# Two small guards of an attention and gated-MLP kernel change engines: GpSimd to VectorE

## The chip, the cores and the metric

The kernel runs on one core of a Trainium2 chip. The metric is device time in microseconds (us) of one execution. The engines of a core run beside each other, each through its own queue in order: TensorE (matrix products), VectorE, ScalarE, GpSimd, and SyncE, which issues the DMA transfers.

## The reference

Attention over 8 batches of 8 heads, 576 positions and 64 channels, where each position sees itself and the 63 before it; then a gated two-layer network whose gate is a 3-tap convolution along the sequence.

```python
scores = scale * np.matmul(q, k.transpose(0, 1, 3, 2))
mask = (rel >= 0) & (rel < 64)
scores = np.where(mask, scores, -1000000000.0)
attn = np.exp(scores - np.max(scores, axis=-1, keepdims=True))
attn = attn / (np.sum(attn, axis=-1, keepdims=True) + 1e-09)
x = np.matmul(attn, v)          # heads put side by side: (8, 576, 512)
h = np.maximum(x @ w_in, 0.0)   # (8, 576, 1024)
conv_out = conv_w[0] * h[s-1] + conv_w[1] * h[s] + conv_w[2] * h[s+1]
out = (h * sigmoid(conv_out)) @ w_out
```

The weights arrive as 64-bit floats and are turned into 32-bit ones on the chip.

## The kernel before

The 4608 positions are worked in 12 units of 384. A unit has three blocks of scores (`softmax(u, b, ...)`): TensorE makes the scores (`qk`, L350), VectorE masks them and takes the row maxima (`row_max`, L357), ScalarE the exponentials with their sums (`exps`, L367), then the sums get 1e-9 added (`guard`, L370), VectorE takes reciprocals (L373) and the scores are normalised (L378). In units 0 and 1 TensorE transposes the result (`transpose_pe`, L384) and ScalarE copies it out (`untile`, L389). `attend` multiplies with v (L481) and splits the result into two parts of reduced float (`xh`, `xl`, L485 and L488); `moe` does the two layers with three products each (L501, L564).

The weights come in chunks: w_in in pieces 0 and 1 of 128x512 alone, then pairs (2, 3), (4, 5), (6, 7) of 128x1024, and w_out in pairs. Each chunk runs through `weights` and `to_f32`: a load (L264), the absolute value on ScalarE (L248), a lower bound TINY so that the exponent has a floor (L249), a shift on VectorE (L250), the sign (L252), the low word on ScalarE (L255), its addition (L256), a rounded copy on GpSimd (L269), and the remainder on VectorE (L270). A buffer half is loaded again when L256 of its former chunk is done. `weights_conv` puts the small convolution weights through the same steps.

The order on every engine is written by a planner, `queued`, when the program is built. Each piece of work has a due time, a cost in us, and the data that it reads and writes. The planner goes through time and gives each engine, of the works that are ready, the one with the lowest due time:

```python
start = max(free[e], min(x.ready for x in ws))
...
x = min((x for x in waiting[e] if x.ready <= start),
        key=lambda x: x.t - (0.5 if x.kind and x.kind == state[e] else 0.0))
...
y.ready = max(y.ready, end + (0.0 if e == "PE" else 0.06) if y.eng == e else end + 0.2)
```

`at` puts down a work, `two` one that takes the port which VectorE and GpSimd have in common for its whole cost in the plan. The due times stand in a table, START: for unit 0 the exponentials of blocks 0, 1, 2 at -42.377, -37.771 and -19.993 (guard and reciprocal 0.45 later, transposes 0.85 later), the first two w_in pieces at -39.031 and -37.38, the pair (2, 3) at -33.878, and unit 1's first scores at -20.012. Where the plan leaves TensorE idle before 110 us, matrix products on a spare tile (L212) are put in.

Of the kernel before, what the change touches and what calls it, by code (L numbers as in the profile page):

```python
# [8 lines left out]
F32 = mybir.dt.float32  # L9
# [3 lines left out]
ALU = mybir.AluOpType  # L13
# [20 lines left out]
TINY = 2.0 ** -15  # L34
# [127 lines left out]
PORT_CL = 0.5  # L162
# [5 lines left out]
def attention_moe(ctx: ExitStack, tc: tile.TileContext, q, k, v, w_in, conv_w, w_out, out):  # L168
    nc = tc.nc
# [48 lines left out]
    def at(t, eng, cost, do, r=(), w=(), kind=None, mb=0, port=0.0):  # L218

        plan.append(Work(t, eng, cost, do, list(r), list(w), kind, mb, port))  # L220

    def two(t, eng, cost, do, **kw):
        at(t, eng, cost, do, port=cost, **kw)
# [17 lines left out]

    def to_f32(t, n, st, x, kb, kt):

        lw, hw, xu = st[..., 0], st[..., 1], x.bitcast(U32)

        at(t, "ACT", 0.0009 * n + 0.2, lambda: nc.scalar.activation(x, hw.bitcast(F32), AF.Abs), r=kb, w=kt)  # L248
        at(t, "POOL", 0.0027 * n + 0.02, lambda: nc.gpsimd.tensor_scalar(x, x, TINY, None, op0=ALU.max), w=kt, port=PORT_CL)  # L249
        two(t, "DVE", 0.00052 * n + 0.06, lambda: nc.vector.tensor_scalar(  # L250
            xu, xu, 3, 0x3FFFFFF8, op0=ALU.logical_shift_left, op1=ALU.bitwise_and), w=kt)
        two(t, "DVE", 0.00104 * n + 0.07, lambda: nc.vector.scalar_tensor_tensor(  # L252
            xu, hw, 0xC0000000, xu, op0=ALU.bitwise_and, op1=ALU.bitwise_or), r=kb, w=kt)

        at(t, "ACT", 0.0009 * n + 0.2, lambda: nc.scalar.activation(lw, lw, AF.Copy, scale=2.0 ** -29), w=kb)  # L255
        two(t, "DVE", 0.00104 * n + 0.07, lambda: nc.vector.tensor_tensor(xu, xu, lw, ALU.add), r=kb, w=kt)  # L256

    def weights(t, src, fs, hi, lo, key, buf, halves):

        e = slice(halves[0] * DM, (halves[-1] + 1) * DM)  # L260
        st, x = bits[buf][:, e], w24[buf][:, e]
        kb, kt = [("bits", buf, a) for a in halves], [("w24", buf, a) for a in halves]
        for f, a, tl in zip(fs, halves, load_at(buf, halves, t)):
            at(tl, "SP", 0.7, lambda f=f, a=a: nc.sync.dma_start(  # L264
                bits[buf][:, a * DM:(a + 1) * DM], src[f].bitcast(U32).rearrange("p (e two) -> p e two", two=2)),
               w=[("bits", buf, a)], mb=0.52)
        n = len(fs) * DM
        to_f32(t, n, st, x, kb, kt)
        two(t, "POOL", 0.00127 * n, lambda: nc.gpsimd.tensor_copy(hi, x), r=kt, w=[f"{key}{f}h" for f in fs])  # L269
        two(t, "DVE", 0.00104 * n + 0.07, lambda: nc.vector.tensor_tensor(lo, x, hi.bitcast(F32), ALU.subtract),  # L270
           r=kt + [f"{key}{f}h" for f in fs], w=[f"{key}{f}l" for f in fs])

    freed = {}

    def load_at(buf, halves, t):

        ts = [freed.get((buf, a), START["bits"][buf][a]) for a in halves]
        for a in halves:
            freed[(buf, a)] = t + 0.01
        return ts  # L280
# [20 lines left out]
    def wide(u):  # L301
        return u < BY_PE

    def place_of(b, i):

        return divmod(NB * b + i, NT)

    def block(u, b, i):

        first = (u * NT + place_of(b, i)[1]) % SB == 0  # L310
        return (P, W if first else 0, 0) if wide(u) else (KW, 0, 2 if first else 1)
# [25 lines left out]
    def bank_keys(u, b):  # L337
        return {1: [("po", 2), ("po", 3)], 2: [("po", 0), ("po", 1)]}.get(b, [("sc", 0)]) if u == 0 else [("sc", 0)]

    def qk(u, b):  # L340
        rows = W if wide(u) else HW
        for i in range(NB):
            g, t0 = place_of(b, i)
            n, o, _ = block(u, b, i)
            for p in range(2):
                for s in range(0, W, rows):
                    r, t = p * W + s, t0 * W + s
                    for h in range(2):
                        hs = slice(h * D, (h + 1) * D)
                        nc.tensor.matmul(banks_of(u, b)[h][r:r + rows, i * P + o:i * P + n], qs[hs, 2 * g + p, t:t + rows],  # L350
                                         ks[hs, 2 * g + p, t + o:t + n], start=True, stop=True)

    def row_max(u, b):
        for i in range(NB):
            n, o, m = block(u, b, i)
            for h in range(2):
                nc.vector.tensor_tensor_reduce(  # L357
                    out=ss[b][:, i, h, o:n], in0=banks_of(u, b)[h][:, i * P + o:i * P + n], in1=mask[m][:, o:n],
                    scale=-0.125, scalar=3.0e38, op0=ALU.add, op1=ALU.min,
                    accum_out=nms[b][:, 2 * i + h:2 * i + h + 1])  # L360

    def exps(u, b, i):
        n, o, _ = block(u, b, i)
        for h in range(2):
            e = slice(2 * i + h, 2 * i + h + 1)
            x = ss[b][:, i, h, o:n]
            nc.scalar.activation(x, x, AF.Exp, bias=nms[b][:, e], scale=-1.0, accum_out=sms[b][:, e])  # L367

    def guard(b, on):
        on.tensor_scalar_add(sms[b], sms[b], 1e-9)  # L370

    def reciprocal(b):
        nc.vector.reciprocal(rs[b], sms[b])  # L373

    def normalise(u, b, on):
        n = P if wide(u) else KW
        sv = ss[b].rearrange("p t h k -> p (t h) k")[:, :, :n]
        on.tensor_tensor(sv, sv, rs[b].unsqueeze(2).broadcast_to([P, 2 * NB, n]), ALU.mult)  # L378
# [40 lines left out]
    def needed(b):  # L419

        keys = []
        for i in range(NB):
            g, t = place_of(b, i)
            n = int(t >= (4, 2)[g])
            keys += [("q", g, n)] + [("k", g, j) for j in range(n + 1)]
        return list(dict.fromkeys(keys))

    def softmax(u, b, t, ex_at):
        at(t, "PE", 0.90 if wide(u) else 0.82, lambda b=b: qk(u, b), r=needed(b), w=bank_keys(u, b),
           kind="tiled" if wide(u) else "eight")  # L430
        for i in range(NB):
            if block(u, b, i)[1]:
                at(t + 0.1, "POOL", 0.2, lambda b=b, i=i: nc.gpsimd.memset(ss[b][:, i, :, :W], 0.0), w=[("s", b, i)])
        at(t + 0.002, "DVE", 1.69 if wide(u) else 1.45, lambda b=b: row_max(u, b),
           r=bank_keys(u, b) + (["mask0"] if wide(u) else ["mask1", "mask2"]), w=[("s", b, i) for i in range(NB)] + [("nm", b)])
        t = ex_at
        for i in range(NB):
            at(t, "ACT", 0.78 if wide(u) else 0.74, lambda b=b, i=i: exps(u, b, i), r=[("nm", b)],
               w=[("s", b, i), ("sm", b, i)], kind="exp")
        t += 0.45  # L440
        sw = [("sm", b, i) for i in range(NB)]
        if u < 3:
            at(t, "POOL", 0.6, lambda b=b: guard(b, nc.gpsimd), w=sw)
        else:
            at(t, "DVE", 0.15, lambda b=b: guard(b, nc.vector), w=sw)
        at(t, "DVE", 0.15, lambda b=b: reciprocal(b), r=sw, w=[("r", b)])
        sr = [("s", b, i) for i in range(NB)]
        if u < 3:
            two(t, "DVE", 1.15 if wide(u) else 0.88, lambda b=b: normalise(u, b, nc.vector), r=[("r", b)], w=sr)
        else:  # L450
            two(t, "POOL", 1.5, lambda b=b: normalise(u, b, nc.gpsimd), r=[("r", b)], w=sr)
        t += 0.4
        if u < BY_PE:
            for j in range(2):
                m, g = ("po", (2 * b + j) % NC), place_of(b, NB // 2 * j)[0]
                at(t, "PE", 0.66, lambda b=b, j=j: transpose_pe(b, j), r=sr + ["mask0"], w=[m])
                at(t + 0.1, "ACT", 0.55, lambda b=b, j=j: untile(b, j), r=[m], w=[("u", g, i) for i in range(4)])
            return
        t = max(t, when[-1][2] + 0.1)
        for g, t0, rows in parts(b):  # L460
            at(t, "DVE", 0.12 * 2 * len(rows), lambda b=b, g=g, t0=t0, rows=rows: transpose(b, g, t0, rows), r=sr,
               w=[("T", g)] + [("bits", i, a) for i in T_BITS[g] for a in range(2)])
            if t0 + len(rows) == NT:
                if u == BY_PE:
                    at(t + 0.01, "POOL", 1.0, lambda g=g: zero_blocks(g), w=[("u", g, i) for i in range(4)])
                for i in range(4):
                    at(t + 0.05, "SP", 2.1, lambda g=g, i=i: place(g, i), r=[("T", g)], w=[("u", g, i)], mb=0.15)
# [263 lines left out]
```

## Time and profile before

| what | us |
|---|---|
| median of 3 runs | 532.17 (531.51 to 532.33) |
| the profiled execution | 531.34 |
| its span, first to last instruction | 529.6 |
| TensorE matmul busy | 518.5 |
| VectorE busy | 380.3 |
| ScalarE busy | 379.7 |
| GpSimd busy | 112.6 |

Busy time is a sum over the whole span, so it says little about one stretch: TensorE's includes the products on the spare tile. In the rows below, times are us from the span's start unless marked ns; PE is TensorE, PEld its weight loads, DVE is VectorE, ACT ScalarE, POOL GpSimd, SP SyncE; L249 is line 249 of the kernel.

### The profile page before, as it was taken

The numbers are of one execution on the slowest core, as the hardware profiler recorded it, in microseconds if no ns is written. First come the engines' busy times: TensorE is split into PE (matmuls) and PEld (weight loads), VectorE is DVE, ScalarE is ACT, GpSimd is POOL, SyncE is SP. The second block draws the span as 40 slices with busy tenths as digits, with TensorE's granted clock in tenths as the row PEclk, the third lists the DMA queues.
The fourth block names the chain that finished last, engine by engine and source line by source line (L and its number), as shares of the span: only waits on it lengthen the run. The fifth ranks groups of instructions, "written<-read, shape, count | busy, mean of one in ns | idle before, by whom it ended". The sixth has DMA issues, their size and how long they took to land.

```text
span 529.6 us, 14836 instructions
## 1 busy us (share of the span) xinstructions
PE 518.5 (98%) x5826; PEld 499.8 (94%) x5826; DVE 380.3 (72%) x1084; ACT 379.7 (72%) x1011; POOL 112.6 (21%) x196
## 2 busy tenths in 40 slices
PE   9998999999999999999999999999999999999996
PEld 8887889999999999999999999999999999999996
DVE  3899999985858667767767767767767667655552
ACT  2997897579896696696697687687687687544542
POOL 6664467113131011021021021021021021000000
PEclk9999999999999999999999999999999999999999
DMA  8984660237292173183083074073073053010011
GB/s 284 365 296 136 208 231 1 60 109 248 76 325 72 58 256 83 42 291 77 21 297 77 16 253 122 21 285 105 13 264 120 17 152 104 16 61 0 2 60 62
DMA packets 29463, 69.98 MB, mean 132 GB/s; under 512 B 5713, under 2 KB 17617, under 8 KB 29393
## 3 DMA queue, kind: packets, MB, share of 16 engines
q1 hardware_dynamic: 29392, 69.03, 39.7%
q8 instruction: 46, 0.75, 0.6%
q14 instruction: 25, 0.20, 0.1%
HBM read 47.73 MB, written 9.47 MB: 108 GB/s over the span
## 4 chain that ended last, share of the span: by engine, by line
PE 85%; DVE 9%; DMA 1%; ACT 1%; issue 1%; SPq 1%; POOL 0%; DVEq 0%
PE po L564 39%; PE acc L501 36%; PE acc L481 6%; PE sc L350 5%; DVE c L535 1%; DVE w L252 1%; DMA T<-in_w_in_dram 1%; DVE s L357 1%; DVE w L256 1%; DVE wil L270 1%; ACT s L367 1%; SPq L234 1%; DVE xl L488 1%; DVE s L378 1%; DVE w L250 1%
## 5 line engine op out<-in xcount | busy, mean ns | idle before, releaser
L501 PE MATMUL acc<-xh,wih 128*128 128x384 f32 x384 | 131.5, 342 | 0.8 <-DVE xl L488 0.8
L564 PE MATMUL po<-gh,woh 128*128 128x386 f32 (+1 forms) x384 | 132.1, 344 | 0.0
L535 DVE SCALAR_TENSOR_TENSOR c<-hbuf,cw,c 128x386 f32<-128x386 f32 (+1 forms) x192 | 109.6, 623 | 30.7 <-ACT c L528 30.7
L564 PE MATMUL po<-gh,wol 128*128 128x386 f32 (+1 forms) x384 | 129.9, 338 | 0.0
L564 PE MATMUL po<-gl,woh 128*128 128x386 f32 (+1 forms) x384 | 129.7, 338 | 0.0
L501 PE MATMUL acc<-xh,wil 128*128 128x384 f32 x384 | 129.7, 338 | 0.0
L501 PE MATMUL acc<-xl,wih 128*128 128x384 f32 x384 | 129.7, 338 | 0.0
L367 ACT ACTIVATE s<-s,nm 128x96 f32<-128x96 f32 (+2 forms) x288 | 105.1, 367 | 5.2 <-DVE nm L357 4.9
L555 DVE TENSOR_TENSOR gl<-c,gh 128x772 fp32r<-128x772 f32 (+1 forms) x48 | 55.8, 1162 | 28.2 <-ACT gh L551 28.1
L501 PEld LDWEIGHTS acc<-xh,wih 128*128 128x128 f32 x384 | 72.1, 188 | 2.9 <-POOL sm L370 0.7
L564 PEld LDWEIGHTS po<-gh,woh 128*128 128x128 f32 x384 | 72.2, 188 | 2.6
L378 POOL TENSOR_TENSOR s<-s,r 128x768 f32<-128x768 f32 x27 | 39.7, 1472 | 163.5 <-DVE r L373 150.7
L547 DVE TENSOR_TENSOR c<-c,hbuf 128x772 f32<-128x772 f32 (+1 forms) x48 | 47.4, 987 | 36.9 <-ACT c L542 36.7
L564 PEld LDWEIGHTS po<-gl,woh 128*128 128x128 f32 x384 | 72.3, 188 | 0.0
L564 PEld LDWEIGHTS po<-gh,wol 128*128 128x128 f32 x384 | 72.3, 188 | 0.0
L501 PEld LDWEIGHTS acc<-xh,wil 128*128 128x128 f32 x384 | 72.2, 188 | 0.0
L501 PEld LDWEIGHTS acc<-xl,wih 128*128 128x128 f32 x384 | 72.1, 188 | 0.0
L522 ACT ACTIVATE hbuf<-acc 128x384 f32<-128x384 f32 x64 | 30.9, 486 | 45.8 <-PE acc L501 45.4
L542 ACT ACTIVATE c<-c 128x772 f32<-128x772 f32 (+1 forms) x48 | 40.7, 848 | 30.2 <-DVE c L535 29.9
L357 DVE CUSTOM_DVE_ANT_0 s<-sc,mask 128x96 f32<-128x96 f32 (+2 forms) x272 | 51.5, 254 | 9.7 <-POOL mask L321 5.7
L367 ACT ACTIVATION_READ_ACCUMULATOR s<-s,nm 128x1 f32 x288 | 54.3, 189 | 0.0
L511 POOL COPY hbuf<-hbuf 128x4 f32<-128x4 f32 x44 | 16.7, 379 | 176.3 <-DVE c L547 176.2
(64 smaller groups left out, 644.5 us busy)
## 6 DMA issues: line engine op xcount, KB each, us to landing
v<-in_v_dram SPq DMA_DIRECT2D x24, 768.0 KB, 7.2
ub<-T SPq DMA_DIRECT2D x240, 48.0 KB, 1.9
k<-in_k_dram SPq DMA_DIRECT2D x22, 448.0 KB, 4.9
q<-in_q_dram SPq DMA_DIRECT2D x22, 384.0 KB, 6.9
out_dram<-T SPq DMA_DIRECT2D x8, 772.0 KB, 4.2
T<-in_w_in_dram SPq DMA_DIRECT2D x8, 512.0 KB, 6.6
T<-in_w_out_dram SPq DMA_DIRECT2D x8, 512.0 KB, 4.2
out_dram<-T SPq DMA_DIRECT2D x3, 768.0 KB, 6.4
```

Of the source, the lines that this page charges most:

```text
L350: nc.tensor.matmul(banks_of(u, b)[h][r:r + rows, i * P + o:i * P + n], qs[hs, 2 * g + p, t:t + rows], ks[hs, 2 * g + p, t + o:t + n], star ...
L357: nc.vector.tensor_tensor_reduce(out=ss[b][:, i, h, o:n], in0=banks_of(u, b)[h][:, i * P + o:i * P + n], in1=mask[m][:, o:n], scale=-0.125 ...
L367: nc.scalar.activation(x, x, AF.Exp, bias=nms[b][:, e], scale=-1.0, accum_out=sms[b][:, e])
L378: on.tensor_tensor(sv, sv, rs[b].unsqueeze(2).broadcast_to([P, 2 * NB, n]), ALU.mult)
L481: nc.tensor.matmul(acc[bank(("v", u, c))][h * D:(h + 1) * D, t * W:(t + 1) * W], vs[:, c, t, h], ub[g][:, 2 * p:2 * p + 2, 2 * t + h], sta ...
L501: nc.tensor.matmul(acc[bank(("m", u, f))][:, :NX], w[:, f, c], x[u % 2][:, c], start=(c == 0 and j == 0), stop=(c == NC - 1 and j == 2))
L522: nc.scalar.activation(hbuf[:, f, o:o + NX], ps[:, :NX], AF.Relu)
L535: nc.vector.scalar_tensor_tensor(c, hbuf[:, f, e:e + n], cw[:, e, f:f + 1], c, op0=ALU.mult, op1=ALU.add)
L542: nc.scalar.activation(c, c, AF.Sigmoid)
L547: nc.vector.tensor_tensor(c, c, hbuf[:, 2 * i:2 * i + 2, 1:1 + n], ALU.mult)
L555: nc.vector.tensor_tensor(gls[ring(u, i)][:, :, :n], cs[i % 2][:, :, :n], ghs[ring(u, i)][:, :, :n].bitcast(F32), ALU.subtract)
L564: nc.tensor.matmul(po[o][:, :n], w[:, f, es], x, start=(f == 0 and j == 0), stop=(f == NF - 1 and j == 2))
```

## The change

The 1e-9 of unit 0's three blocks, and the lower bound TINY of the two w_in pieces that are converted alone, are done by VectorE. Units 1 and 2 keep GpSimd for the 1e-9 (the later units had VectorE already), and the other chunks keep GpSimd for TINY. The costs given to the planner go with the engines; all due times stay. Since the order is planned from costs, the order of other works may come out otherwise too.

```diff
-    def to_f32(t, n, st, x, kb, kt):
+    def to_f32(t, n, st, x, kb, kt, early=False):
...
-        at(t, "POOL", 0.0027 * n + 0.02, lambda: nc.gpsimd.tensor_scalar(x, x, TINY, None, op0=ALU.max), w=kt, port=PORT_CL)
+        if early:
+            two(t, "DVE", 0.00052 * n + 0.06, lambda: nc.vector.tensor_scalar(x, x, TINY, None, op0=ALU.max), w=kt)
+        else:
+            at(t, "POOL", 0.0027 * n + 0.02, lambda: nc.gpsimd.tensor_scalar(x, x, TINY, None, op0=ALU.max), w=kt, port=PORT_CL)
...
-        to_f32(t, n, st, x, kb, kt)
+        to_f32(t, n, st, x, kb, kt, len(fs) == 1)
...
-        if u < 3:
+        if 0 < u < 3:
             at(t, "POOL", 0.6, lambda b=b: guard(b, nc.gpsimd), w=sw)
         else:
             at(t, "DVE", 0.15, lambda b=b: guard(b, nc.vector), w=sw)
```

## Rows read from the trace of the kernel before

**Rows 1.** Busy time by stretch: length, each engine's busy time (instructions), clock, DMA.
```profile
12.30:19.25 6.95, 6.23 (x80) 6.01 (x79) 3.89 (x8) 6.95 (x31) 2.98 (x4) 1.00 1.04 410
19.25:38.40 19.15, 18.11 (x320) 16.35 (x317) 18.97 (x68) 18.67 (x66) 13.71 (x13) 1.00 0.86 301
38.40:75.84 37.44, 33.35 (x453) 30.52 (x454) 37.41 (x89) 31.79 (x84) 20.00 (x16) 1.00 0.60 198
```

**Rows 2.** TensorE's waits from 76 us on: total, times, longest.
```profile
PE acc L501 <- DVE xl L488: 0.2, 1, 0.2
```

**Rows 3.** Timeline 12 to 19 us: start, length, engine, line, operation.
```profile
12.29 0.67 ACT L248 ACTIVATE w<-T 128x512 f32<-128x512 f32 x1 [4.56 <-DMA T<-in_w_in_dram]
...
13.05 1.49 POOL L249 TENSOR_SCALAR w<-w 128x512 f32<-128x512 f32 x1 [2.97 <-ACT w L248]
...
14.57 0.43 DVE L250 TENSOR_SCALAR w<-w 128x512 uint32<-128x512 uint32 x1 [2.14 <-POOL w L249]
...
15.03 0.69 DVE L252 SCALAR_TENSOR_TENSOR w<-T,w 128x512 uint32<-128x512 uint32 x1
15.07 0.19 ACT L367 ACTIVATION_READ_ACCUMULATOR s<-s,nm 128x1 f32 x1
...
15.34 0.50 POOL L370 TENSOR_SCALAR sm<-sm 128x8 f32<-128x8 f32 x1 [0.80 <-ACT s L367]
...
15.87 0.20 DVE L373 RECIPROCAL r<-sm 128x8 f32<-128x8 f32 x1
...
16.10 1.22 DVE L378 TENSOR_TENSOR s<-s,r 128x1024 f32<-128x1024 f32 x1
...
17.25 0.68 DVE L256 CUSTOM_DVE_ANT_0 w<-T,w 128x1024 uint16<-128x1024 uint16 x1
...
17.77 1.00 PE L350 MATMUL sc<-k,q 64*64 64x128 f32 x32 [0.72 <-DMA q<-in_q_dram]
...
18.64 0.69 DVE L270 TENSOR_TENSOR wil<-w,wih 128x512 fp32r<-128x512 f32 x1 [0.71 <-POOL wih L269]
...
18.70 1.09 PE L384 MATMUL po<-ident,s 128*128 128x128 f32 x8
```

**Rows 4.** Timeline 18 to 29 us, three engines, by engine.
```profile
18.69 0.68 ACT L248 ACTIVATE w<-T 128x512 f32<-128x512 f32 x1
...
19.88 1.16 ACT L248 ACTIVATE w<-T 128x1024 f32<-128x1024 f32 x1
20.94 0.57 ACT L389 COPY ub<-po 128x512 f32<-128x512 f32 x1
...
21.12 2.96 POOL L249 TENSOR_SCALAR w<-w 128x1024 f32<-128x1024 f32 x1
...
19.25 0.28 DVE L357 CUSTOM_DVE_ANT_0 s<-sc,mask 128x128 f32<-128x128 f32 x1
...
20.80 0.08 DVE L357 DVE_READ_ACCUMULATOR2_ANT nm<- 128x1 f32 x1
21.03 0.43 DVE L250 TENSOR_SCALAR w<-w 128x512 uint32<-128x512 uint32 x1
...
21.49 1.41 DVE L252 SCALAR_TENSOR_TENSOR w<-T,w 128x512 uint32<-128x512 uint32 x1
22.82 1.21 DVE L378 TENSOR_TENSOR s<-s,r 128x1024 f32<-128x1024 f32 x1
...
23.95 0.68 DVE L256 CUSTOM_DVE_ANT_0 w<-T,w 128x1024 uint16<-128x1024 uint16 x1
...
29.06 1.21 DVE L256 CUSTOM_DVE_ANT_0 w<-T,w 128x2048 uint16<-128x2048 uint16 x1
```

**Rows 5.** Timeline at 123 us, VectorE: a later unit's guard and reciprocal.
```profile
123.05 0.16 DVE L370 TENSOR_SCALAR sm<-sm 128x8 f32<-128x8 f32 x1
123.24 0.20 DVE L373 RECIPROCAL r<-sm 128x8 f32<-128x8 f32 x1
```

**Rows 6.** Timeline at 38 us, VectorE: a later normalisation.
```profile
38.20 2.06 DVE L378 TENSOR_TENSOR s<-s,r 128x1024 f32<-128x1024 f32 x1
```

More of the change, by code (lines that the diff above doesn't have):

```diff
@@ L267, in weights @@
         n = len(fs) * DM
-        to_f32(t, n, st, x, kb, kt)
-        two(t, "POOL", 0.00127 * n, lambda: nc.gpsimd.tensor_copy(hi, x), r=kt, w=[f"{key}{f}h" for f in fs])
-        two(t, "DVE", 0.00104 * n + 0.07, lambda: nc.vector.tensor_tensor(lo, x, hi.bitcast(F32), ALU.subtract),
-           r=kt + [f"{key}{f}h" for f in fs], w=[f"{key}{f}l" for f in fs])
+        to_f32(t, n, st, x, kb, kt, len(fs) == 1)
+        his, los = [f"{key}{f}h" for f in fs], [f"{key}{f}l" for f in fs]
+        two(t, "POOL", 0.00127 * n, lambda: nc.gpsimd.tensor_copy(hi, x), r=kt, w=his)
+        two(t, "DVE", 0.00104 * n + 0.07, lambda: nc.vector.tensor_tensor(lo, x, hi.bitcast(F32), ALU.subtract), r=kt + his, w=los)
     freed = {}
```

## The prediction

> **What bounds the kernel now.** I read the busy time by stretch first [rows 1]. From 19.25 us to 38.40 VectorE works 18.97 of 19.15 us, and from 38.40 to 75.84 it works 37.41 of 37.44, so it is full. Before that, from 12.30 to 19.25, it works only 3.89 of 6.95 us. TensorE's granted clock is 1.00 in all three, the upper of its two levels (2.4 GHz), so the clock is no term here. Then I read TensorE's waits behind 76 us: there is one, 0.2 us long, for VectorE [rows 2]. So the start-up is set by VectorE until about 76 us, and then TensorE alone sets the pace. A change that lies before 42 us, as this one does, can only move the moment at which TensorE becomes free of VectorE; microseconds won before it must survive a full VectorE queue.
>
> Third, the order of time around the first weight chunk [rows 3]. ScalarE starts its absolute value at 12.29, GpSimd's guard runs from 13.05 for 1.49 us, and VectorE, which has been idle for 2.14 us, goes on at 14.57. The first score block's sums are complete at 15.07 + 0.19 = 15.26; GpSimd guards them from 15.34 and VectorE's reciprocal starts at 15.87. Fourth, the same around the second chunk [rows 4].
>
> **The first chunk's exponent.** Removed: 1.49 us of GpSimd. Added: a VectorE tensor_scalar over 128x512 with one constant. No row shows it in float; the nearest is the shift at L250, same shape and engine, which lets the next instruction go 0.34 us after it (21.03 to 21.37) [rows 4]. Bounds: 0.34, and 0.69 if it ran as slowly as the two-input L252 [rows 3]; I take 0.34. It starts where GpSimd did (13.05), so the shift goes from 14.57 to 13.39, and L252 ends near 14.4 instead of 15.7. That 1.2 us is worth nothing by itself: what VectorE has to do next is the sums' guard, and ScalarE delivers those at 15.26 as before. The later chain is set by the normalisation.
>
> **The first block's sums.** A guard on VectorE with the reciprocal behind it takes 0.19 us from start to start (123.05 to 123.24) [rows 5]. From the same 15.34: reciprocal at 15.53 instead of 15.87, normalisation at 15.76 instead of 16.10. Gain: 0.34 us, bounded by 0 and the 0.53 that GpSimd's part takes now (15.34 to 15.87). Everything tied to it follows: L256 at 16.91, and with the 1.39 us from L256 to L270 (17.25 to 18.64, GpSimd's cast between them), L270 at 18.30, out of the way 0.61 later at 18.91.
>
> **What that does to the written order.** The planner takes, of the works that are ready, the one with the earliest due time. The transposes of block 0 are due at -41.5, the scores of unit 1's block 0 at -20.0. In the run TensorE took the scores first, at 17.77, when their q had landed, and the transposes at 18.70 [rows 3]. The normalisation now takes 0.15 + 0.15 + 1.15 by its costs instead of 0.6 + 0.15 + 1.15, and one allowance of 0.2 for a hop between engines becomes 0.06: 0.59 sooner by the planner's clock. I worked its rule through by hand: the transposes become ready just ahead of the load (by 0.1 on its clock, which serves here for the order alone). So I expect the transposes first, from about 17.0 to 18.1, and the scores right behind. Then VectorE finds block 1's sums (at 18.87, as now, because ScalarE's exponentials don't move) ready before unit 1's scores, and does guard, reciprocal and normalisation of block 1 ahead of the row maxima; now they stand at 21.37 and 22.82, behind them.
>
> **The second chunk.** On VectorE, by the same row distances: guard 18.91, reciprocal 19.10, normalisation 19.33, out at 20.48 (1.15, as 16.10 to 17.25); row maxima 1.63 (19.25 to 20.88), out at 22.11; exponent guard 22.45; shift 22.79; L252 with 0.62 unhindered, 23.41. At present the same work, the normalisation at 22.82 included, is out at 23.95 [rows 4]. Lead: 0.54 us. GpSimd's wait at 21.03 bought nothing before: VectorE was in the row maxima until 20.88, so its removal is worth 0.15 at most.
>
> **The port.** At 21.12 GpSimd starts its guard of chunks 2 and 3, and L252 at 21.49 takes 1.41 us instead of 0.69 [rows 3, 4]: 0.72 lost. A normalisation that starts just behind such a guard takes 2.06 instead of 1.21 [rows 6, 3]. With both copies of unit 0's block 0 (0.47 each, 20.94 to 21.41 in spacing) now ahead of ScalarE's two absolute values, that guard starts near 21.47. L252 was freed at 21.12 + 1.09; the same would hold VectorE to 22.56, and the new guard at 22.11 could lose 0 to 0.45. No row has a one-input VectorE instruction beginning under a GpSimd instruction, so I keep both and take 0.2 between. What reads against a dearer collision is the normalisation at 22.82: it began inside the 2.96 us of the GpSimd guard (21.12 to 24.08) and took its plain 1.21 [rows 4]. The Trainium skill, "SBUF — State Buffer", section "Who interferes with whom", says that a VectorE instruction in a two-port mode or with two SBUF inputs and a GpSimd instruction exclude each other for the whole of the one that issued first. By it that normalisation would have stood until 24.08; the row disagrees. By the rule the sum below would grow by some 2 us; by the row it does not.
>
> **From 23.41 on.** The same set of work up to the end of unit 1's second row maxima takes 23.95 to 29.06 now, 5.11 us [rows 4]. It gains the third block's guard, 0.19; its GpSimd form lay beside other work, so nothing on VectorE pays for it. The lead is 0.54 - 0.2 - 0.19 = 0.15, between -0.1 (full collision) and 0.35 (none). The third chunk and the rest keep their code. L256 of chunk 1 probably falls behind the second row maxima, so its buffer's reload on SyncE's queue and, one in-order queue on, chunk 4's absolute value come nearly 1 us later. The plan can fill that gap on ScalarE with exponentials. Without that cover the late value would cost VectorE up to the same 1 us.
>
> **Sum.** The profiled execution took 531.34 us (span 529.6 and 1.7 around it), the median of the three runs is 532.17, 0.83 above. 531.34 - 0.15 = 531.2 for the profiled one, 532.17 - 0.15 = 532.0 for the median. About 1.06 us (0.2%) is what a measurement of this kernel can tell from no change.
>
> **The rivals.** *No lead at all*: the transposes stay behind the scores. Then the row maxima still wait for qk, the second chunk's guard falls at 20.9 and L252 meets GpSimd at the same place; 0.19 for the third guard remains: 532.2 to 532.4. For it: the margin of 0.1. Chance 0.10. *Faster*: the shifted queues miss collisions that are there now. Each is worth 0.72 to 0.85 [rows 4, 6]; the full lead of 0.35 with one or two of them is -1.2 to -2.05, 530.1 to 531.0. For it: VectorE is full, so each stall lost there comes through; against it: GpSimd waits for the same VectorE and ScalarE results, so its starts move along. Chance 0.27. *Slower by the order*: the due times belong to the old durations. It is the reload of chunk 1's buffer: if ScalarE's queue has chunk 4's absolute value ahead of unit 1's exponentials, all behind it comes up to 1 us later, and one more collision of 0.85 follows when GpSimd's guard meets a normalisation; +1.5 to +1.9, 533.7 to 534.0. It decides once the delay exceeds the time that VectorE has other ready work. Chance 0.23. *Slower by the port*: the new fast instruction at 22.11 stands until the GpSimd guard that began at 21.47 has ended, 2.96 us on, at 24.43: 2.32 lost, less 0.35 of lead, 534.1. Beside it stands the skill's page named above; the row at 22.82 speaks against it, though it has another shape. Chance 0.08.
>
> **How the numbers follow.** Forecast 0.32 and no lead 0.10 make 0.42 within 0.2%; faster 0.27; slower 0.23 + 0.08 = 0.31. The forecast's own range is 531.3 to 532.9, with the bounds of the lead and one collision either way cut at the threshold. The range takes in both sides: from 530.1, two collisions missed, to 534.0, the reload and one collision; what is beyond it is most of the port case and a third collision.
>
> **What the changed profile would show.** The first shift near 13.4; the first reciprocal near 15.5; L384 ahead of unit 1's first L350 on TensorE; block 1's normalisation before 19.5; a VectorE guard near 22.1 of 0.34 to 0.8 us; the second L256 after L357 of unit 1's second block. VectorE still full from 20 to 76 us, and TensorE's last wait for VectorE near 75.7. I would be wrong if VectorE gets holes behind 24 us, if the new guard lasts above 2 us, if TensorE's order changes between 38 and 76 us so that it waits in other places, or if the transposes stay behind the scores and still something moves.

## The result, and the profile after

The changed kernel took 533.64 us (median of 13 runs) beside 532.17 for the kernel before; the ratio is 1.0032, with a 95% interval from 1.0023 to 1.0042. One of the 13 runs of the kernel before took 1749.32 us and is not in the ratio, which compares the runs that agree. So the change is slower, by 1.5 us by the medians and by some 1.7 by the ratio. The range on record (530.1 to 534.0) holds it; the forecast "within 0.2%" does not.

The profiled execution took 533.82 us. Lines behind the edit have moved by one to four: L250 is the new lower bound on VectorE, L253 the shift (L250 before), L255 the sign (L252), L259 the addition of the low word (L256), L274 the remainder (L270), L353 the scores (L350), L360 the row maxima (L357), L370 the exponentials (L367), L373 the guard (L370), L381 the normalisation (L378), L387 the transposes (L384), L484 the product with v (L481), L491 `xl` (L488), L504 and L567 the two layers (L501, L564), L521 and L525 ScalarE's copies of the first layer's output out of PSUM (L518, L522), L538 the convolution (L535), L558 the low part `gl` that the second layer reads (L555). `nm` are the row maxima, `wil` and `wol` the remainders of w_in and w_out.

First the place of the edit. Timeline of the changed kernel, 13 to 32 us, VectorE: start, length, engine, line, operation.

```profile
13.60 0.43 DVE L250 TENSOR_SCALAR w<-w 128x512 f32<-128x512 f32 x1 [0.48 <-ACT w L248]
14.06 0.43 DVE L253 TENSOR_SCALAR w<-w 128x512 uint32<-128x512 uint32 x1
...
15.90 0.17 DVE L373 TENSOR_SCALAR sm<-sm 128x8 f32<-128x8 f32 x1 [0.69 <-ACT s L370]
16.11 0.20 DVE L376 RECIPROCAL r<-sm 128x8 f32<-128x8 f32 x1
16.42 1.23 DVE L381 TENSOR_TENSOR s<-s,r 128x1024 f32<-128x1024 f32 x1
17.56 0.68 DVE L259 CUSTOM_DVE_ANT_0 w<-T,w 128x1024 uint16<-128x1024 uint16 x1
...
20.00 1.23 DVE L381 TENSOR_TENSOR s<-s,r 128x1024 f32<-128x1024 f32 x1
21.14 0.42 DVE L250 TENSOR_SCALAR w<-w 128x512 f32<-128x512 f32 x1
21.48 0.28 DVE L360 CUSTOM_DVE_ANT_0 s<-sc,mask 128x128 f32<-128x128 f32 x1
...
23.03 0.42 DVE L253 TENSOR_SCALAR w<-w 128x512 uint32<-128x512 uint32 x1
23.49 0.69 DVE L255 SCALAR_TENSOR_TENSOR w<-T,w 128x512 uint32<-128x512 uint32 x1
...
27.21 0.58 DVE L373 TENSOR_SCALAR sm<-sm 128x8 f32<-128x8 f32 x1
27.71 1.21 DVE L255 SCALAR_TENSOR_TENSOR w<-T,w 128x1024 uint32<-128x1024 uint32 x1
...
31.11 1.21 DVE L259 CUSTOM_DVE_ANT_0 w<-T,w 128x2048 uint16<-128x2048 uint16 x1
```

The new bound frees the shift 0.46 us after it starts, not 0.34, and the guard frees the reciprocal after 0.21. (In this execution ScalarE began the first absolute value at 12.90, 0.61 later than in [rows 3]; read distances here, not start times.) Block 1's normalisation stands at 20.00, ahead of the row maxima, and L255 takes 0.69 where it took 1.41 [rows 4]. Up to here it goes much as forecast. TensorE's timeline confirms the other step on which the forecast rested, transposes ahead of scores:

```profile
17.79 1.06 PE L387 MATMUL po<-ident,s 128*128 128x128 f32 x8 [0.29 <-DVE s L381]
18.79 1.00 PE L353 MATMUL sc<-k,q 64*64 64x128 f32 x32
```

Now where the time went. I counted how many weight products of the two layers TensorE had started by a given time (instructions of L504 and L567, of L501 and L564 before; all 2304 are in each trace). Between 90 and 110 us the kernel before starts 114 of them in 20 us, so one is worth 0.175 us. The last column counts the instructions on the spare tile (L212) between 50 and 110 us, which stand where the plan leaves TensorE idle. The five lower rows are experiments, told below.

| kernel | by 50 us | by 66 | by 90 | by 110 | spare products |
|---|---|---|---|---|---|
| before | 33 | 72 | 179 | 293 | 40 |
| after | 48 | 72 | 177 | 286 | 62 |
| e2: order of after, engines of before | 48 | 72 | 178 | 286 | 62 |
| e1: engines of after, order of before | 30 | 72 | 176 | 290 | 40 |
| e5: before, one planned cost changed | 36 | 72 | 166 | 273 | 66 |
| e11: before, other due times | 48 | 89 | 209 | 312 | 28 |
| e12: the same order, engines of after | 37 | 84 | 203 | 310 | 28 |

At 50 us the changed kernel is 15 products ahead (2.6 us); at 66 it is level, at 110 it is 7 behind (1.2 us). So the loss does not come from the edit's own place; it comes behind 50 us. The starts of single products, later (+) or earlier (-) than in the kernel before, show its parts (one execution each, from TensorE's timelines; e7 and e10 are experiments that repair the first part):

| weight product | before, us | after | e2 | e1 | e7 | e10 |
|---|---|---|---|---|---|---|
| 37th | 50.62 | -3.72 | -3.52 | +0.48 | -3.05 | -4.60 |
| 241st | 100.80 | +0.35 | +0.25 | +0.49 | +0.02 | -1.70 |
| 301st | 111.38 | +1.25 | +1.15 | +0.50 | +0.96 | -0.06 |
| 541st | 165.97 | +2.43 | +2.45 | +0.46 | +2.12 | +1.09 |

From the 541st on the changed kernel stays some 2.4 us late, which is the difference of the two spans (532.0 and 529.6). First its lead is used up. Then 0.9 us go before the 301st product, where six spare products stand that the kernel before doesn't have:

```profile
103.25 0.82 PE L212 MATMUL acc<-spare 128*128 128x112 f32 x6
```

The last 1.2 us go between the 301st and the 541st, where TensorE waits in neither kernel: these 240 products take 54.6 us in the kernel before and e1, and 55.7 to 55.9 in the changed kernel, e2 and e7 to e10, which have its order of TensorE there. The same eight sets of products with v and five of scores stand among them in nine groups instead of six. No experiment shows whether changing between these kinds of product costs the whole 1.2 us.

For the first part, the windows of the changed kernel show the stretch from 40 us on (length, busy time of PE, PEld, DVE, ACT, POOL with their instructions, TensorE's clock, DMA share, GB/s):

```profile
40.00:54.00 14.00, 13.15 (x148) 11.63 (x148) 13.97 (x33) 13.72 (x32) 6.61 (x5) 1.00 0.32 98
54.00:58.00 4.00, 2.38 (x89) 1.81 (x83) 4.00 (x21) 1.39 (x4) 2.11 (x1) 0.94 0.48 193
58.00:62.00 4.00, 4.00 (x18) 4.00 (x18) 4.00 (x6) 3.98 (x8) 0.65 (x3) 0.64 0.76 211
62.00:66.00 4.00, 4.00 (x59) 3.72 (x65) 4.00 (x21) 4.00 (x10) 3.23 (x2) 1.00 0.54 215
```

TensorE's own timeline says what happens between 54 and 66 us:

```profile
54.52 0.47 PE L212 MATMUL po<-spare 128*128 128x112 f32 x2
56.62 1.32 PE L353 MATMUL sc<-k,q 64*32 64x96 f32 x64 [1.62 <-DVE nm L360]
57.87 0.69 PE L504 MATMUL acc<-xh,wih 128*128 128x384 f32 x1
58.36 0.52 PE L504 MATMUL acc<-xh,wil 128*128 128x384 f32 x1
58.68 0.52 PE L504 MATMUL acc<-xl,wih 128*128 128x384 f32 x1
...
61.45 1.26 PE L212 MATMUL po<-spare 128*128 128x112 f32 x10
```

It waits 1.62 us for row maxima. Behind the wait, twelve products take 57.87 to 61.45, 0.30 us each instead of 0.175: the granted clock has gone to its lower level (0.64 on average in that window). Then come spare products, because the plan has nothing ready. VectorE's timeline shows what it waits for: four steps of the convolution (51.56, 3.77 us) stand ahead of the row maxima. It also shows two works that have become late: the remainder of the chunk (6, 7), 57.73 now and 51.81 before, and an `xl` of unit 1. Three of the four `xl` were done at 70.1 before and the last came at 75.24; now two are done at 66.5, and the other two come at 74.53.

```profile
51.56 3.77 DVE L538 SCALAR_TENSOR_TENSOR c<-hbuf,cw,c 128x386 f32<-128x386 f32 x4
55.25 0.25 DVE L360 CUSTOM_DVE_ANT_0 s<-sc,mask 128x96 f32<-128x96 f32 x1
...
57.73 1.21 DVE L274 TENSOR_TENSOR wil<-w,wih 128x1024 fp32r<-128x1024 f32 x1
...
71.54 1.23 DVE L259 CUSTOM_DVE_ANT_0 w<-T,w 128x2048 uint16<-128x2048 uint16 x1 [1.31 <-ACT T L258]
72.68 1.93 DVE L538 SCALAR_TENSOR_TENSOR c<-hbuf,cw,c 128x386 f32<-128x386 f32 x2
74.53 1.01 DVE L491 TENSOR_TENSOR xl<-acc,xh 128x384 fp32r<-128x384 f32 x2
```

The same places in the kernel before, VectorE and then TensorE:

```profile
51.81 2.05 DVE L270 TENSOR_TENSOR wil<-w,wih 128x1024 fp32r<-128x1024 f32 x1
53.78 1.14 DVE L535 SCALAR_TENSOR_TENSOR c<-hbuf,cw,c 128x386 f32<-128x386 f32 x2
54.85 0.25 DVE L357 CUSTOM_DVE_ANT_0 s<-sc,mask 128x96 f32<-128x96 f32 x1
...
69.13 1.01 DVE L488 TENSOR_TENSOR xl<-acc,xh 128x384 fp32r<-128x384 f32 x2
...
75.24 0.55 DVE L488 TENSOR_TENSOR xl<-acc,xh 128x384 fp32r<-128x384 f32 x1
...
53.57 0.41 PE L501 MATMUL acc<-xh,wih 128*128 128x384 f32 x1
56.22 1.16 PE L350 MATMUL sc<-k,q 64*32 64x96 f32 x64 [0.31 <-DVE nm L357]
```

The row maxima begin only 0.40 us later than before (55.25 and 54.85). The wait is long because TensorE is early: the twelve products that it had for this time before (from 53.57) are already done. So the lead of 15 products ends here, because VectorE does not bring the row maxima forward. GpSimd has a part in that, by the new order: two of the convolution's steps take 1.10 us at 48.27, the four take 3.77 while GpSimd rounds the chunk (6, 7) and guards the next one (timeline of the changed kernel, GpSimd):

```profile
51.70 1.37 POOL L273 CAST wih<-w 128x1024 fp32r<-128x1024 f32 x1 [6.43 <-DVE w L259]
53.03 3.08 POOL L252 TENSOR_SCALAR w<-w 128x1024 f32<-128x1024 f32 x1
```

The convolution's due times (1.5, 3.5, 5.5) are far later than the chunk's (-12); it stands ahead because the planner takes only works that are ready. The remainder needs GpSimd's rounded copy of its chunk, which ran at 49.77 before and runs at 51.70 now, when VectorE is free and the convolution ready.

### The profile page after: what moved, and what is told of

It is laid out like the page before. It is cut to its first block, busy times and chain, and to the rows that moved or that the text cites. A ratio compares the mean times of both kernels' runs of the same rounds, so it can differ in the third digit from the quotient of the medians.

```text
span 532.0 us, 14850 instructions
## 1 busy us (share of the span) xinstructions
PE 522.6 (98%) x5836; PEld 502.7 (94%) x5836; DVE 380.3 (71%) x1089; ACT 379.7 (71%) x1011; POOL 105.4 (20%) x191
## 4 chain that ended last, share of the span: by engine, by line
PE 89%; DVE 7%; DMA 1%; SPq 1%; ACT 1%; issue 0%; POOL 0%; DVEq 0%
PE po L567 39%; PE acc L504 37%; PE acc L484 6%; PE sc L353 5%; DMA T<-in_w_in_dram 1%; DVE s L381 1%; DVE s L360 1%; PE po L212 1%; DVE c L538 1%; DVE w L259 1%; SPq L234 1%; DVE wil L274 1%; DVE w L255 1%; ACT s L370 0%; DVE xl L491 0%
## 5 line engine op out<-in xcount | busy, mean ns | idle before, releaser
L538 DVE SCALAR_TENSOR_TENSOR c<-hbuf,cw,c 128x386 f32<-128x386 f32 (+1 forms) x192 | 111.5, 633 | 31.0 <-ACT c L531 31.0
L504 PE MATMUL acc<-xh,wih 128*128 128x384 f32 x384 | 132.3, 345 | 1.2 <-ACT hbuf L525 0.6
L567 PE MATMUL po<-gh,woh 128*128 128x386 f32 (+1 forms) x384 | 132.3, 345 | 0.0
L504 PE MATMUL acc<-xh,wil 128*128 128x384 f32 x384 | 130.5, 340 | 0.0
L504 PE MATMUL acc<-xl,wih 128*128 128x384 f32 x384 | 130.2, 339 | 0.0
L567 PE MATMUL po<-gh,wol 128*128 128x386 f32 (+1 forms) x384 | 130.0, 338 | 0.0
L567 PE MATMUL po<-gl,woh 128*128 128x386 f32 (+1 forms) x384 | 129.9, 338 | 0.0
L370 ACT ACTIVATE s<-s,nm 128x96 f32<-128x96 f32 (+2 forms) x288 | 105.1, 367 | 6.0 <-DVE nm L360 5.8
L504 PEld LDWEIGHTS acc<-xh,wih 128*128 128x128 f32 x384 | 72.7, 189 | 3.8 <-issue 1.1
L558 DVE TENSOR_TENSOR gl<-c,gh 128x772 fp32r<-128x772 f32 (+1 forms) x48 | 54.9, 1144 | 28.6 <-ACT gh L554 28.6
L567 PEld LDWEIGHTS po<-gh,woh 128*128 128x128 f32 x384 | 72.3, 188 | 2.6
L381 POOL TENSOR_TENSOR s<-s,r 128x768 f32<-128x768 f32 x27 | 39.7, 1471 | 168.6 <-DVE r L376 168.6
L567 PEld LDWEIGHTS po<-gl,woh 128*128 128x128 f32 x384 | 72.4, 188 | 0.3 <-DVE gl L558 0.3
L504 PEld LDWEIGHTS acc<-xh,wil 128*128 128x128 f32 x384 | 72.6, 189 | 0.0
L504 PEld LDWEIGHTS acc<-xl,wih 128*128 128x128 f32 x384 | 72.6, 189 | 0.0
L567 PEld LDWEIGHTS po<-gh,wol 128*128 128x128 f32 x384 | 72.4, 188 | 0.0
L525 ACT ACTIVATE hbuf<-acc 128x384 f32<-128x384 f32 x64 | 30.9, 483 | 40.5 <-PE acc L504 40.5
L360 DVE CUSTOM_DVE_ANT_0 s<-sc,mask 128x96 f32<-128x96 f32 (+2 forms) x272 | 51.6, 255 | 11.3 <-PE sc L353 11.2
L531 ACT ACTIVATE c<-hbuf,cw 128x386 f32<-128x386 f32 (+1 forms) x96 | 53.6, 608 | 1.2 <-DVE gl L558 1.2
L370 ACT ACTIVATION_READ_ACCUMULATOR s<-s,nm 128x1 f32 x288 | 54.4, 189 | 0.0
```

The costliest lines, as they stand in the source:

```text
L360: nc.vector.tensor_tensor_reduce(out=ss[b][:, i, h, o:n], in0=banks_of(u, b)[h][:, i * P + o:i * P + n], in1=mask[m][:, o:n], scale=-0.125 ...
L504: nc.tensor.matmul(acc[bank(("m", u, f))][:, :NX], w[:, f, c], x[u % 2][:, c], start=(c == 0 and j == 0), stop=(c == NC - 1 and j == 2))
L525: nc.scalar.activation(hbuf[:, f, o:o + NX], ps[:, :NX], AF.Relu)
L531: nc.scalar.activation(cs[i % 2][:, a, :n], hbuf[:, f, 1:1 + n], AF.Copy, scale=cw[:, 1, f:f + 1])
L538: nc.vector.scalar_tensor_tensor(c, hbuf[:, f, e:e + n], cw[:, e, f:f + 1], c, op0=ALU.mult, op1=ALU.add)
L558: nc.vector.tensor_tensor(gls[ring(u, i)][:, :, :n], cs[i % 2][:, :, :n], ghs[ring(u, i)][:, :, :n].bitcast(F32), ALU.subtract)
```

## The experiments

Theory A: the engines are worth nothing that can be told; the loss is the other order that the planner writes from the new costs. Theory B: the work itself on VectorE costs it (a full engine, or the port shared with GpSimd). Each kernel was timed in five rounds beside the kernel before, whose median was 531.28 us in e1 to e4, 531.68 in e5 to e8, 531.82 in e9 to e11 and 531.53 in e12; medians below are therefore compared by their ratios to it.

**e1: the engines without the order.** VectorE does the three kinds of work, but the planner is still given GpSimd's cost and queue, so every other work keeps its place. (e2 is the reverse: the planner is told VectorE, the instruction is issued by GpSimd.)

```diff
         if early:
-            two(t, "DVE", 0.00052 * n + 0.06, lambda: nc.vector.tensor_scalar(...), w=kt)
+            at(t, "POOL", 0.0027 * n + 0.02, lambda: nc.vector.tensor_scalar(...), w=kt, port=PORT_CL)
...
-        if 0 < u < 3:
-            at(t, "POOL", 0.6, lambda b=b: guard(b, nc.gpsimd), w=sw)
+        if u < 3:
+            at(t, "POOL", 0.6, lambda b=b: guard(b, nc.gpsimd if u else nc.vector), w=sw)
```

> VectorE does the five guards, but the planner is still given GpSimd and GpSimd's costs for them, so every queue keeps the order of before. Theory A (the order is what costs): not slower than before, 531.2 to 532.4 in the median, VectorE's remainder of w_in chunk (6, 7) done near 54 us as before, TensorE's clock 1.00 throughout. Theory B (five more instructions on a full VectorE and their meetings with GpSimd at the port cost): 533 to 534, with VectorE falling behind before by about 1 us from 21 us on.

531.74 us, ratio 1.0006 (0.9997 to 1.0016): no difference that can be told. The timeline of e1, VectorE, shows why nothing was won either: the second chunk's shift now meets GpSimd's guard of the chunks (2, 3) (0.92 us instead of 0.43), and L259 starts at 24.14, where it started at 23.95 [rows 4].

```profile
21.44 0.92 DVE L253 TENSOR_SCALAR w<-w 128x512 uint32<-128x512 uint32 x1
22.29 0.19 DVE L376 RECIPROCAL r<-sm 128x8 f32<-128x8 f32 x1
22.40 0.69 DVE L255 SCALAR_TENSOR_TENSOR w<-T,w 128x512 uint32<-128x512 uint32 x1
23.01 1.22 DVE L381 TENSOR_TENSOR s<-s,r 128x1024 f32<-128x1024 f32 x1
24.14 0.68 DVE L259 CUSTOM_DVE_ANT_0 w<-T,w 128x1024 uint16<-128x1024 uint16 x1
```

**e2: the order without the engines.**

> The planner is given the change's engines and costs, so every queue has the order of after, but GpSimd does the five guards as before. Theory A (the order): slower than before by at least what the change costs, 533.6 to 535.5, the more because GpSimd's 1.5 us guards stand in a plan made for 0.3 us. Theory B (VectorE's load): as before, 531.5 to 532.5.

533.53 us, ratio 1.0042 (1.0029 to 1.0055): the whole loss, with all the moved guards on GpSimd. In the two tables above its counts and delays are nearly those of the changed kernel, and the wait for the row maxima is the same (TensorE's waits from 30 to 130 us in e2: total, times, longest):

```profile
PE sc L353 <- DVE nm L360: 1.6, 1, 1.6
```

e1 and e2 together decide for Theory A: the order is enough to make the loss, the engines are not.

**e3 and e4: one half of the change each**, engines and planned costs together: e3 moves the sums' guards alone, e4 the exponents' bounds alone.

```diff
e3:  -        to_f32(t, n, st, x, kb, kt, len(fs) == 1)
e3:  +        to_f32(t, n, st, x, kb, kt)
e4:  -        if 0 < u < 3:
e4:  +        if u < 3:
```

> Only the three sums' guards of unit 0 move to VectorE, in cost and engine. Theory A: this alone brings the transposes of block 0 ahead of unit 1's scores and the normalisation of block 1 ahead of the row maxima, so the w_in chunk (6, 7) is late again and the time is 533 to 535. Theory C (the first chunk's exponent, 1.2 us sooner, is what upsets the order): as before, 531.5 to 532.5.

> Only the lower bounds of w_in chunks 0 and 1 move to VectorE, in cost and engine. Theory A: the first sums still decide when block 0 is normalised, so the first 20 us keep the order of before; 531.7 to 532.7. Theory C: the order breaks here, 533 to 535.

e3: 533.2 us, 1.0031 (1.0021 to 1.0041). One detail of Theory A is not there: the remainder of the chunk (6, 7) came at 50.67, as early as before, so that late piece is not a necessary part of the loss. e4: 534.95 us, 1.0064 (1.005 to 1.0077). Under Theory A I had expected little of it; it is slower than the whole change. The theory was right that the order decides, and I was wrong on which edit disturbs it. Both halves break the order, each in another way, and their losses do not add up to that of the whole.

**e5: no engine moved at all.** The kernel before, with the planner told that unit 0's guard on GpSimd costs 0.5 us instead of 0.6 (it takes 0.50 for the first block [rows 3], and 0.55 and 1.10 for the other two).

```diff
-            at(t, "POOL", 0.6, lambda b=b: guard(b, nc.gpsimd), w=sw)
+            at(t, "POOL", 0.5 if u == 0 else 0.6, lambda b=b: guard(b, nc.gpsimd), w=sw)
```

> The kernel before, every operation on its old engine; only the planner's cost for unit 0's guard on GpSimd is 0.5 instead of 0.6, a tenth of a microsecond in the plan. Theory A (the due times fit one set of costs, and any other order that they give is worse): slower than before by 1.5 to 4 us, with the queues in another order from the first guard on. Theory D (the changed engines' order alone is bad, a nudge of costs is harmless): as before, within 0.6 us.

535.69 us, 1.008 (1.0067 to 1.0093), 4 us slower by 0.1 us in one planned cost. Its spare products rise to 66. The due times fit one set of costs; another set, though truer for the first block, loses microseconds.

**e6: the change with other due times.** A search tries due times in START one after another and keeps those with which the written plan ends sooner.

```diff
-    "sig": ((3.087, 7.079, 8.764, 10.751), ...
-    "in": (-39.031, -37.38, -33.878, -12.682, -12.013),
+    "sig": ((5.041, 7.079, 8.764, 8.969), ...
+    "in": (-39.031, -37.38, -33.878, -14.293, -12.377),
...
```

> The change with other due times, found by a search on the planner's own clock with the change's costs; the operations and the data flow are those of the change. Theory A: the loss is a matter of due times, so it goes away: no slower than before, 528.5 to 531.5, with the w_in chunk (6, 7) back before 55 us. Theory B (the moved instructions cost VectorE time that no order gives back): still 1 us or more above before, 532.3 and up.

529.34 us, 0.996 (0.9946 to 0.9973): faster than both kernels. But the remainder of the chunk (6, 7) still came at 57.22, and TensorE still waited 1.57 us at 56.11; so this order does not repair what I had found late, and the expectation that it would is wrong. The gain comes behind 58 us, where weight products fill what spare products held. Whether the change or the search earns it is the question of e11.

**e7: the hole at 55 us filled**, that is, the 1.62 us in which TensorE waits for the row maxima. Seven spare products (14 instructions in the trace) in place of one where the plan is at 55.3.

```diff
-            n = int((start - t) * FILL)
+            n = 7 if 55.2 < t < 55.4 else int((start - t) * FILL)
```

> The change, with seven spare products instead of one where TensorE stands 1.6 us before unit 2's third scores, so that it stays busy there. If the lowered clock behind that hole (the granted clock was 0.64 in 58 to 62 us) is a part of the loss, it stays at 1.00 and the time falls by 0.4 to 1.3 us against the change: 532.0 to 533.0. If the clock is no part, the time stays or grows by up to 0.3 us, and a low clock shows elsewhere or none did cost.

532.56 us, 1.0017 (1.0008 to 1.0026). TensorE's wait for `nm` shrinks from 1.62 to 0.26 us, the clock is 1.00 in all windows from 54 to 80 us, and about half of the loss is gone, though the spare products do no work. So part of it was the low clock behind the wait, as far as the intervals tell, which just overlap with those of the changed kernel. In its profiled execution the 241st product is level with the kernel before; the two later parts of the loss are there as in the changed kernel (0.94 and 1.16 us).

**e8 and e9: the stretch behind 66 us.** e8 puts no spare products behind 66 us of the plan; e9 adds one edit, the two `xl` of unit 1 moved ahead of the convolution's works due 5.5 in VectorE's queue.

```diff
e8:  -FILL, FILL_FROM, FILL_TO = 4.0, 2.0, 110.0
e8:  +FILL, FILL_FROM, FILL_TO = 4.0, 2.0, 66.0
...
e9:  -        for x in queued(plan, keep_busy):
e9:  +        order = queued(plan, keep_busy)
e9:  +        los = [x for x in order if x.w in ([("xl", 1, 0)], [("xl", 1, 3)])][:2]
e9:  +        for x in los:
e9:  +            order.remove(x)
e9:  +        i = next(i for i, x in enumerate(order) if x.eng == "DVE" and x.t == 5.5)
e9:  +        order[i:i] = los
e9:  +        for x in order:
```

> The change without the spare products that the planner puts in behind 66 us of its clock: 18 rows near 69 us and 6 near 103 us. If these products hold up work that is ready (the remainder of w_out's first chunk is done at 69.2 us and its first product starts at 71.2), the time falls by 0.6 (those near 103 alone) to 2.5 us against the change. If they only fill waits, it stays, and an idle TensorE may lower the clock and cost 1 us more.

> The kernel of e8_no_late_filler with one edit of order more: the two VectorE splits of unit 1's values c0 and c3 (xl, the low parts that the weight products of unit 0's f=6 and f=7 read) stand in VectorE's queue right before the first work of the conv whose due time is 5.5, instead of behind it and behind the second exponents. Theory (TensorE at 70 to 75 us is short of work because these two splits come at 74.5 us while their inputs are ready at 69.8): TensorE's wait of 1.85 us at 75.4 us for xl goes, the granted clock of 74 to 80 us comes back from 0.72 to 1.00, and the time falls by 1.3 to 2.5 us against e8, to 531.0 to 532.2 us. Rival (the late splits only show where TensorE has run dry; something else before 66 us sets it): the wait moves to another tile and the time stays at 533.2 to 533.8 us.

e8: 533.47 us, 1.0037 (1.0024 to 1.005), nothing won. The second layer starts at 69.5 instead of 71.2, but what the spare products had covered comes out as a wait for the late `xl` (TensorE, timeline of e8), and the clock goes to 0.72 in the window 74 to 80:

```profile
75.45 0.44 PE L504 MATMUL acc<-xh,wih 128*128 128x384 f32 x1 [1.85 <-DVE xl L491]
```

e9: 532.4 us, 1.0017 (1.0005 to 1.0029), 1.07 less than e8. The `xl` now stand at 69.92, that wait is gone and the clock of 74 to 80 us is 1.00. So the late `xl` are a second part, again with intervals that just overlap. The gain is a little below the 1.3 to 2.5 expected: in the profile of e9 TensorE waits later instead, 0.98 us at 97.00 for `gl`, and 1.38 at 104.65 for ScalarE's copy out of PSUM, where the changed kernel has its six spare products:

```profile
97.00 0.44 PE L567 MATMUL po<-gl,woh 128*128 128x386 f32 x1 [0.98 <-DVE gl L558]
104.65 0.45 PE L504 MATMUL acc<-xh,wih 128*128 128x384 f32 x1 [1.38 <-ACT hbuf L521]
```

**e10: both repairs**, the filled hole of e7 and the order of e9.

> e9_splits_first with the hole at 55 us filled as in e7_hole_filled (7 spare products in the place of 1). Theory (the hole with its low clock and the late splits are two separate losses that add up): e7 was worth 1.1 us, so e10 comes out about 1.1 us under e9, at 530.0 to 531.2 us, under the kernel before's 531.7. Rival (both are the same microseconds of slack of TensorE, lost once): e10 is within 0.4 us of e9.

532.65 us, 1.0023 (1.0012 to 1.0033): no faster than e9. The expectation that two losses add up is wrong. The hole's wait is down to 0.27 us here, but TensorE waits 1.16 at 68.71 for the remainder of a w_out chunk, 0.45 at 95.10 for `gl`, and 1.39 at 102.75 for ScalarE's copy. What is repaired early is taken back later: the 241st product starts 1.70 us ahead of the kernel before, the 301st level with it (that last wait), the 541st 1.09 us behind (the order of TensorE, as in the changed kernel). So what e9 and e10 leave of the loss lies behind 100 us.

**e11: the control of e6.** The kernel before, guards on GpSimd, with due times from the same search.

```diff
-    "bits": ((-46.561, -47.419), (-44.383, -45.007)),
-    "qk1": -43.011,
+    "bits": ((-46.561, -47.419), (-44.383, -47.12)),
+    "qk1": -44.246,
...
-    "ex0": (-42.377, -37.771, -19.993),
+    "ex0": (-42.377, -34.695, -19.993),
...
```

> The kernel before, guards on GpSimd as they were, with other due times found by the same search that gave e6_change_retimed its own (planner's end 527.2 in both). It is the control of e6, which ran in 529.34 us beside 531.68 of the kernel before. Theory (the gain of e6 is that of the due times; the engine of the three guards is worth little by itself): 529.0 to 530.0 us, within 0.4 us of e6. Rival (the guards on VectorE are themselves worth the lead of 1 to 2 us that the trace shows at 40 us): 530.5 to 532 us.

527.05 us, 0.9923 (0.9905 to 0.9941), better than e6 by 2 us and outside both expectations (529.0 to 530.0, and 530.5 to 532). So e6's gain is no merit of the change: due times alone give more. The windows say where it comes from. This one answers to the last of [rows 1]:

```profile
38.40:75.84 37.44, 35.14 (x458) 31.81 (x458) 37.41 (x89) 34.21 (x90) 21.19 (x16) 1.00 0.55 187
```

VectorE is as full as before (37.41 us); TensorE works 1.8 us more under it, and 28 spare products instead of 40 stand behind 50 us. The convolution ahead of unit 2's row maxima is two steps long, as before, instead of four in the changed kernel, and TensorE's wait there is 0.93 us (timeline of e11, TensorE):

```profile
53.37 1.16 PE L350 MATMUL sc<-k,q 64*32 64x96 f32 x64 [0.93 <-DVE nm L357]
```

**e12: e11's order, the guards on VectorE.** To e11 what e1 is to the kernel before: the two edits of e1 put into e11.

> The order of e11_before_retimed (its due times, and the planner still given GpSimd's costs for the three guards), with the guards carried out by VectorE: to e11 what e1_engines_old_order is to the kernel before. Theory (the engine of the three guards is worth nothing that can be told, in a good order too): 526.6 to 528.0 us, within 0.2% of e11's 527.05. Rival 1 (in a plan whose start-up loses little, the lead of the first two chunks comes through): 525.5 to 526.4 us. Rival 2 (VectorE, full in this stretch, pays for the guards, or they break the fine order again): 528.5 to 531 us.

527.23 us beside e11's 527.05; the ratios to the kernel before are 0.9914 (0.99 to 0.9927) and 0.9923 (0.9905 to 0.9941). The engine of these guards is worth nothing that can be told in this order either.

## Why the prediction was wrong, and where it was right

**Half right: what bounds the kernel.** In the kernel before VectorE is full up to 76 us, then TensorE alone sets the pace, and the faster e11 has done more on TensorE under a full VectorE. Wrong is that the change "can only move the moment at which TensorE becomes free of VectorE": 2.1 of the 2.4 us between the two profiles go behind 100 us, in TensorE's own order. Nor does VectorE stay full: it waits 1.31 us for ScalarE at 71.54, one of the signs named against the forecast.

**Right, nearly in number: the place of the edit.** The guard with its reciprocal behind costs 0.21 us (0.19 forecast); the bound frees VectorE after 0.46 behind the first chunk and 0.34 behind the second (0.34 forecast for both). The transposes come ahead of unit 1's scores, block 1's normalisation ahead of the row maxima, the second L259 behind unit 1's second row maxima (26.01). The second bound runs at 21.14, ahead of the row maxima, where I had it behind them, at 22.11.

**Half right: the port.** I took 0.2 us of collision at the second bound, between 0 and 0.45. It met no GpSimd instruction: that guard started only at 22.07. The third block's guard met one: 0.50 us from it to the next instruction (27.21 to 27.71), under GpSimd's cast (26.76, 1.00 us), instead of 0.19; it ends at 27.79, with the cast. In e1 a shift that begins under GpSimd's guard takes 0.92 us instead of 0.43, but it doesn't stand for the guard's whole 2.77. The rival "slower by the port" falls: nothing waited 2 us, and e2 has the loss without any new VectorE instruction.

**Wrong: "From 23.41 on."** The step that failed is the sentence that the third chunk and the rest keep their code, and with it the assumption that a lead or lag of VectorE at 29 us is passed on as it is. The code is kept; the order is not. I had worked the planner's rule through by hand for the first two chunks, where it turned out well, and let it stand for everything behind. The same rule exchanges works on all engines behind them: two more steps of the convolution get ahead of unit 2's row maxima (a wait of 1.62 us and, in this execution, a lower clock behind it), others ahead of an `xl`, and TensorE has six spare products at 103 us and another order up to 166. The term of the sum, -0.15 us, should have been "the engines nothing, the order +1.7", as e1 (1.0006) and e2 (1.0042) show. The planner itself would have told the sign: by the clock on which the plans of e6 and e11 end at 527.2, that of the kernel before ends at 528.6 and that of the changed kernel at 532.1 (e3 532.8, e4 532.7, e5 534.8; worked out by running `queued` on the works of each kernel).

**The rivals.** "Slower by the order" (chance 0.23, 533.7 to 534.0) had the cause in kind (due times that belong to old durations) and nearly the time, but not the mechanism, so that the time is near is luck: I had put it at the reload of chunk 1's buffer, ScalarE's absolute value and one more collision. The third chunk is indeed later (L259 at 31.11, 29.06 in [rows 4]), yet TensorE is 15 products ahead at 50 us, so that delay is not where the time was lost. "Faster" counted collisions missed; one was missed (L255, 0.72 us), and it didn't come through. "No lead" falls with the transposes. Among the signs that would prove me wrong I had named a changed order of TensorE between 38 and 76 us; that is what came.

**Open.** Hole with low clock (e7) and late `xl` (e8 to e9) are parts worth 0.0015 and 0.002 of the ratio, each at the edge of what the intervals tell; they do not add up (e10). The traces place the rest behind 100 us, but no experiment repairs the place at 103 us or TensorE's order from 111 to 166, so what each is worth alone is not shown.

## What to carry to other kernels

Where a planner writes the order from costs, an edit of a cost is an edit of the whole order behind it: hold the order fixed to learn what the engine is worth (e1, e12), and issue the old instructions in the new order to learn what the order is worth (e2). Compare the ends of the two plans before the first run: here they gave the sign. If hand-tuned due times were found for one set of costs, search them again before judging a change, and give the kernel before the same search (e11), or the search's gain is put down to the change. A lead of TensorE far ahead of the end, here 15 products at 50 us, says nothing by itself; look where the plan next leaves it without work, and compare the start of the same product, far behind the edit, in both traces.

## What was not expected of the hardware

The same wait does not always cost the same. TensorE stood about 1.6 us for row maxima in the changed kernel, e2, e6, e8 and e9; the granted clock behind it went to the lower level in two of these profiles (0.64 in 58 to 62 us; 0.81 and 0.76 in e9) and stayed at 1.00 there in the other three. It stayed at 1.00 behind e1's wait of 1.70 us at 44.68 too. Of the 13 runs of the changed kernel, the five with a mean clock of 1.000 have a median of 533.21 us, the other eight 533.84. The difference, 0.6 us, is about what the clock costs in the runs that have it. The kernel before isn't free of it: of its 79 runs beside the experiments 44 have a mean clock below 1.000, with a median of 531.81 us beside 531.46. So the clock is a small part of the loss: the five at 1.000 are still 1 us above the 532.17 of the kernel before. In the profiled execution of e12 it is a shorter pair of waits behind which the clock is lower, 1.17 and 0.67 us with 1.16 us of scores between them: the products behind it come 0.32 us apart until 49.8 us (TensorE's timeline of e12):

```profile
44.43 1.16 PE L353 MATMUL sc<-k,q 64*32 64x96 f32 x64 [1.17 <-DVE nm L360]
46.25 0.52 PE L504 MATMUL acc<-xh,wih 128*128 128x384 f32 x1 [0.67 <-ACT hbuf L525]
46.57 0.52 PE L504 MATMUL acc<-xh,wil 128*128 128x384 f32 x1
```
